# Matrix-product weights that begin 32 bytes later in SBUF, and two parts of the moving operand in swapped places

## The chip, the core and the metric

One core of a Trainium2 chip runs the whole program. TensorE (PE in the profile; its weight loads are listed apart as PEld) multiplies, VectorE (DVE), ScalarE (ACT) and GpSimd (POOL) do the elementwise work, SyncE (SP) issues transfers. The metric is device microseconds for one execution.

A matrix product on PE has two operands in SBUF: the weights (`lhsT`), which a weight load brings into the array before the product starts, and the moving operand (`rhs`), which streams through it, one column after the other. The weights of the next product are loaded while the present one streams, so two places of SBUF are read at a time.

## The reference

```python
def sm_attn(qq, kk, vv):
    s = scale * np.matmul(qq, kk.transpose(0, 1, 3, 2))
    s = s - np.max(s, axis=-1, keepdims=True)
    a = np.exp(s)
    a = a / (np.sum(a, axis=-1, keepdims=True) + 1e-09)
    return np.matmul(a, vv)
p_packed = sm_attn(p, k, v)          # p: (8, 8, 32, 64); q, k, v: (8, 8, 576, 64)
x = sm_attn(q, p_packed, p_packed)   # heads are then put side by side: (8, 576, 512)

h = x.transpose(0, 2, 1) @ U @ V     # U: (576, 32), V: (32, 576)
u = x + h.transpose(0, 2, 1)
out = u + np.maximum(u @ w_ch1, 0.0) @ w_ch2    # w_ch1: (512, 2048), w_ch2: (2048, 512)
```

## The kernel before

The work has an opening, in which the eight batches' packed keys and values are attended to, weights are read and converted, and batches 0 and 1 are begun; then a stage for batch 1; then a loop over batches 2 to 7, whose steps are written out in order (`prologue`, `batch_steps`, `joint_steps`, each word a step). The order on every engine is the order of these lists: nothing is scheduled behind the author's back. Each round of the loop computes the attention of the next batch beside the two large products of the present one.

**First product.** `half1` (L781) computes a piece of the hidden layer: for each of the two groups of heads, g = 0 and 1, three products by `mm3` (L98). Every number is split into a high and a low float32r part, and high x high, high x low, low x high are added; they stand at L100, L101 and L102. The weights are `wh` and `wl` (tiles `wth`, `wtl`, three buffers each), the moving operand is the attention weights `ah`, `al` (two buffers each). A tile of a is 1,152 numbers long and holds four parts: for each g 320 columns (r = 0) and 256 columns (r = 1). `part` (L90) gives the place of each. L419 and L441 are the two small products that mix U and V in (`ua4` and `ms` as weights, `x`, `xh` and `vs` as moving operand).

**Second product.** For batch 0 and 1 `tile2` (L817) multiplies the hidden layer `h` as weights by `w2h`, `w2l`, 512 columns at a time, again at L100 to L102. From batch 2 on a scheme with seven products in place of eight is used: `Sweep.products` and `Sweep.add` (L1054), all at L1058, 256 columns at a time, with weights `h` and moving operands `w2h`, `w2l` and the sums `ta`, `tb`, `tc`, `td`, `te` and, late, `x`.

**Places in SBUF.** Tiles come from pools in the order in which they are asked for, each rounded up to 32 bytes. Four tiles named `gap0` to `gap3` are never used; they only take room, so that what follows begins at a chosen place. SBUF is full to the last 32 bytes. Start of a tile in bytes of the partition, and its remainder by 128, as built:

| Tile | Part in the products | Start | mod 128 |
|---|---|---|---|
| `wth`, `wtl` (3 + 3 buffers) | weights of the first product | 121,280 (first) | 64 |
| `h` (2) | weights of the second | 165,312 (first) | 64 |
| `ah`, `al` (2 + 2) | moving, first product | 146,816 (first) | 0 |
| `w2h0` and the other seven | moving, second | 58,752 (first) | 0 |
| `ta`, `tb`, `tc`, `td`, `te`, `x` | moving, second | all | 0 |
| `ua4`; `ms` | weights of L419; of L441 | 21,120; 145,792 | 0 |
| `xT` (with `xh`, `xJ` in its place) | moving in L321, L419; source rows | 133,568 | 64 |
| `e` (softmax of the second attention) | not read by PE | 138,688 | 64 |
| `e1` (in the trace `e`) | weights of the transposes L327 | 216,544 (first) | 96 |
| `ident` | moving in all transposes | 16,512 | 0 |

Every single weight matrix begins a multiple of 512 bytes behind its tile's start, so the remainder is the same for all of them.

**Softmax of the second attention.** `side`, `most`, `each`, `power`, `total` and `back` (L359 to L387): DVE finds the maxima over 32 numbers (L367), POOL subtracts them (L371), ACT takes the exponential, DVE the sums (L379), POOL multiplies by their reciprocals (L371 again). Maxima and sums have a tile each, `m` and `s`, of 18 numbers.

Of the kernel before, what the change touches and what calls it, by code (L numbers as in the profile page):

```python
# [9 lines left out]
F32 = mybir.dt.float32  # L10
# [10 lines left out]
def packed_attention_mixer_kernel(  # L21
# [28 lines left out]
    B, H, S, D = q.shape  # L50
# [4 lines left out]
    P = 128  # L55
# [9 lines left out]
    HALF = (slice(0, 5 * I), slice(5 * I, S))  # L65
# [23 lines left out]

    def part(t, g, r):  # L90
        n = HALF[r].stop - HALF[r].start
        c0 = n * g + (0 if r else 2 * (S - HALF[1].start))
        return t[:, c0:c0 + n]

    def copy(scalar):
# [9 lines left out]
    pipe = ctx.enter_context(tc.tile_pool(name="pipe", bufs=1))  # L105
# [223 lines left out]
            nc.tensor.transpose(t_ps[:I, o:o + P], src[:, LAST], ident)  # L329


    def attention(b, res):

        st = {}
# [28 lines left out]
            nc.vector.transpose(st["e", g][:, (0, 10)[r]:(10, 18)[r]], st["ss", g][r][:, :n])  # L363

        def most(g):
            m = st["m", g] = pipe.tile([P, S // 32], F32, name="m", bufs=1)
            nc.vector.tensor_reduce(m, st["e", g], axis=AX.X, op=ALU.max)  # L367

        def each(g, what, op):
# [5 lines left out]

        def total(g, k):
            if k == 0:
                s = st["s", g] = pipe.tile([P, S // 32], F32, name="s", bufs=1)
                nc.vector.tensor_reduce(s, st["e", g], axis=AX.X, op=ALU.add)  # L379
            elif k == 1:  # L380
                nc.vector.tensor_scalar_add(st["s", g], st["s", g], 1e-9)
            else:
                nc.vector.reciprocal(st["s", g], st["s", g])
# [63 lines left out]
        def high_mix2(g, hf):  # L447
            nc.scalar.copy(part(res[b][0], g, hf), st["aT", g][:, HALF[hf]])  # L448

        def low_mix2(g, hf):  # L450
            (ah, al), aT, ns = (part(t, g, hf) for t in res[b]), st["aT", g], HALF[hf]
            nc.gpsimd.tensor_tensor(al, aT[:, ns], ah.bitcast(F32), op=ALU.subtract)  # L452
# [4 lines left out]
        if b != 2:  # L457
            gh = list(product(range(2), range(2)))
            return {
                "a0": [load], "a1": [run(load_q, 1)],  # L460
                **{f"q{h}": [run(turn_q, g, h) for g in range(2)] for h in range(3)},
                **{f"q{h}a": [lambda scalar, g=g, h=h: turned_q(g, h, scalar) for g in range(2)] for h in range(3)},
                "s3": [run(scores_q, g) for g in range(2)],
                "s4": [run(side, g, r) for g, r in gh],
                "s5": [run(most, g) for g in range(2)],
                "s6": [run(each, g, "m", ALU.subtract) for g in range(2)],
                "s7": [run(power, g) for g in range(2)],
                "s8": [run(total, g, k) for g in range(2) for k in range(3)],
                "s9": [run(each, g, "s", ALU.mult) for g in range(2)],
                "sa": [run(back, g) for g in range(2)],  # L470
                "t0": [room],
                "t1": [run(tokens, k) for k in (0, 2, 4)],
                "t2": [run(split_tokens, k, False) for k in (0, 2, 4)],
                "t3": [run(split_tokens, k, True) for k in (0, 2, 4)],
                "x0": [mix1], "x1": [run(split_mix1, False)], "x2": [run(split_mix1, True)],
                "y0": [run(mix2, g, hf) for hf, g in gh],
                "y1": [run(add_mix2, g, hf) for hf, g in gh],
                "y2": [run(high_mix2, g, hf) for hf, g in gh],
                "y3": [run(low_mix2, g, hf) for hf, g in gh],
                "pu": [put],  # L480
            }
# [10 lines left out]
        def step_most(g):  # L492
            most(g)
            each(g, "m", ALU.subtract)

        def step_total(g):
            for k in range(3):
                total(g, k)
            each(g, "s", ALU.mult)
# [64 lines left out]

    def folded(f_ps, b, c, a, g, low):
        if not wt:
            pipe.tile([P, 16], F32, name="gap3", bufs=1)
        if (b, 2 * c + a) not in wt:
            wt[b, 2 * c + a] = tuple(
                pipe.tile([P, 2, QW // 2], F32R, name=f"wt{x}", tag=f"wt{x}", bufs=3) for x in "hl")  # L570
        hi, lo = wt[b, 2 * c + a]
        src = f_ps[g][:, QW // 2 * a:QW // 2 * a + QW // 2]
        if not low:
            nc.scalar.copy(hi[:, g], src)  # L574
        else:
            nc.vector.tensor_tensor(lo[:, g], src, hi[:, g].bitcast(F32), op=ALU.subtract)  # L576

    def fold(b, c):
        f_ps = fold_products(b, c)
        for a, g, low in product(range(2), range(2), range(2)):  # L580
            folded(f_ps, b, c, a, g, low)
# [80 lines left out]
    def a_back(u, part, bank):  # L662
        t_ps = ua[u]["b_ps", part] = bank()
        for kk in ((0, 1, 2, 3), (4,))[part]:
            turn_back(t_ps, ua[u]["e"], kk, P * (kk % 4))
# [60 lines left out]
    pools, kept = {}, {}  # L726
# [3 lines left out]
    def h_tile():  # L730
        return first_h.pop() if first_h else pools["B"].tile([P, 2, 7 * P], F32R, name="h", bufs=2)

    def close_sA():
        actx.close()
        pools["B"] = ctx.enter_context(tc.tile_pool(name="sB", bufs=2, reuse_waits="tile"))
        pools["B"].tile([P, 16], F32, name="gap0", bufs=1)
        first_h.append(h_tile())
        pools["B"].tile([P, 112], F32, name="gap1", bufs=1)

    def close_psA():  # L740
        pctx.close()
# [408 lines left out]
    def folded_one(n, low):  # L1150
        n, m = divmod(n, 4)
        folded(f00[n], n // NPC, n % NPC, m // 2, m % 2, low)
# [25 lines left out]
    }  # L1178
    stages = {name: map(lambda n, f=f: lambda *args: f(n, *args), count()) for name, f in units.items()}
    side = [attention(b, res) for b in range(2)]  # L1180
    stages.update((name, iter(fs + side[1][name])) for name, fs in side[0].items())
    stages.update((name, iter(fs)) for name, fs in {
# [5 lines left out]
    for word in opening.split():  # L1188
        name = word.rstrip("v") if word not in stages else word
        stage = next(stages[name])  # L1190
        if name in ("e0", "e1", "ge") and not pools:
            close_sA()
        if name == "G0" and "O" not in pools:
            close_psA()
        if name in either:
            stage(name == word)
        else:
            stage()
    ahead = attention(2, res)
    ahead.pop(0)()  # L1200
    steps = ahead
    last = kept["cur"]
    now = Batch(1)
    for kt in range(NK):
# [11 lines left out]
        if kt % 4 == 2:  # L1216
            n = NPC + kt // 4 + 1
# [96 lines left out]
    for x in ("", "n"):  # L1314
# [8 lines left out]
            "S" + x: [lambda f=f: stream_w1((f[1] + 1) % NPC) for f in folds[x] if f != (B - 1, 3)],  # L1323
        })
    coming = [attention(b, res) for b in range(3, B)]
    stages.update({name: [f for a in coming for f in a[name]] for name in coming[0]})
    stages = {name: iter(fs) for name, fs in stages.items()}
# [50 lines left out]
```

## Time and profile before

| What | us |
|---|---|
| Time, median of 3 runs | 767.47 |
| Lowest and highest | 766.36, 768.63 |
| The profiled execution's own time | 768.76 |
| Its span, first to last instruction | 766.4 |

| Engine | Busy us | Share of the span | Instructions |
|---|---|---|---|
| PE | 751.3 | 98% | 7,792 |
| PEld | 662.2 | 86% | 7,792 |
| DVE | 590.3 | 77% | 1,223 |
| ACT | 405.3 | 53% | 1,020 |
| POOL | 84.7 | 11% | 116 |

The mean granted clock of TensorE is 0.998. A group of instructions is given with its line, engine, operation, tiles (out<-in), shape and count, then its busy us and the mean ns of one, then the idle time before it and what ended it. Matrix products overlap, so the mean duration of one (281 ns, say) is longer than the distance at which they follow each other; that distance is read from the chain of waits or the timeline, where a row has a start, a length in us and a count: in the chain a piece's length runs to the start of the next piece.

### The profile page before, as it was taken

How to read it: one execution, taken by the hardware profiler on the slowest of the kernel's cores; microseconds unless marked ns; L12 is line 12 of the kernel's file. 1: busy time of each engine (PE TensorE's matmuls, PEld its weight loads, DVE VectorE, ACT ScalarE, POOL GpSimd, SP SyncE). 2: the span in 40 equal slices, each digit the busy share in tenths (PEclk: the TensorE clock that was granted, in tenths of full speed). 3: DMA queues.
4: the chain of work that ended last, by engine and by line, in shares of the span. 5: the costliest groups of instructions: out<-in, count | busy, mean ns of one | idle time of the engine just before them, and what ended most of it. 6: DMA issues, size and time to landing. Idle time of an engine off the chain costs nothing.

```text
span 766.4 us, 19548 instructions
## 1 busy us (share of the span) xinstructions
PE 751.3 (98%) x7792; PEld 662.2 (86%) x7792; DVE 590.3 (77%) x1223; ACT 405.3 (53%) x1020; POOL 84.7 (11%) x116
## 2 busy tenths in 40 slices
PE   8999999999999999999999999999999999999996
PEld 6666778887878889998999989998999999999996
DVE  4799799877787668867888778857886788755786
ACT  4788755553344645555454544555455555464442
POOL 1123111010101011100211002010201020100000
PEclk9999999999999999999999999999999999999999
DMA  9999985379112874766479474657464746563672
GB/s 319 350 353 303 309 219 155 110 244 283 39 68 74 259 215 139 220 197 200 152 225 255 144 241 139 196 174 238 150 183 172 239 148 178 173 231 104 203 220 74
DMA packets 105689, 151.24 MB, mean 197 GB/s; under 512 B 40448, under 2 KB 59904, under 8 KB 102016
## 3 DMA queue, kind: packets, MB, share of 16 engines
q1 hardware_dynamic: 105440, 149.75, 62.0%
q8 instruction: 61, 1.00, 0.5%
q10 hardware_dynamic: 160, 0.26, 0.1%
q14 instruction: 28, 0.23, 0.1%
HBM read 116.29 MB, written 33.69 MB: 196 GB/s over the span
## 4 chain that ended last, share of the span: by engine, by line
PE 84%; DMA 5%; DVE 5%; ACT 3%; issue 1%; SPq 1%; POOL 0%; ACTq 0%; POOLq 0%; DVEq 0%
PE o L1058 32%; PE h_ps L100 9%; PE h_ps L101 8%; PE h_ps L102 8%; PE t_ps L562 4%; PE o L100 4%; PE o L101 3%; PE o L102 3%; DMA w1s<-w1D 2%; PE t_ps L301 1%; PE o L1080 1%; PE t_ps L321 1%; DMA bits<-in_moe_w_ch_dram 1%; PE t_ps L419 1%; PE t_ps L327 1%
## 5 line engine op out<-in xcount | busy, mean ns | idle before, releaser
L1058 PE MATMUL o<-w2h,h 128*128 128x256 f32 x896 | 178.9, 281 | 0.0
L100 PE MATMUL h_ps<-ah,wth 128*128 128x256 f32 (+1 forms) x512 | 157.6, 308 | 0.8 <-ACT aP L801 0.4
L101 PE MATMUL h_ps<-al,wth 128*128 128x256 f32 (+1 forms) x512 | 150.4, 294 | 0.0
L102 PE MATMUL h_ps<-ah,wtl 128*128 128x256 f32 (+1 forms) x512 | 150.3, 294 | 0.0
L1058 PEld LDWEIGHTS o<-w2h,h 128*128 128x128 f32 x896 | 146.4, 189 | 2.6 <-issue 2.6
L1052 DVE TENSOR_TENSOR h<-bits,h 128x896 fp32r<-128x896 f32 (+1 forms) x112 | 115.4, 1030 | 35.2 <-ACT h L1047 34.4
L1047 ACT CAST h<-bits 128x896 fp32r<-128x896 f32 (+1 forms) x112 | 100.4, 896 | 62.7 <-DVE bits L1035 37.7
L1058 PE MATMUL o<-w2l,h 128*128 128x256 f32 x448 | 125.0, 279 | 0.0
L100 PEld LDWEIGHTS h_ps<-ah,wth 128*128 128x128 f32 x512 | 96.4, 188 | 25.3 <-ACT ppall L1023 9.2
L101 PEld LDWEIGHTS h_ps<-al,wth 128*128 128x128 f32 x512 | 96.4, 188 | 1.0
L102 PEld LDWEIGHTS h_ps<-ah,wtl 128*128 128x128 f32 x512 | 96.4, 188 | 0.0
L1058 PE MATMUL o<-tb,h 128*128 128x256 f32 x504 | 88.0, 282 | 0.4 <-DVE h L1052 0.2
L1023 ACT ACTIVATE bits<-h_ps 128x256 f32<-128x256 f32 x132 | 49.4, 384 | 67.8 <-PE h_ps L102 50.8
L1058 PEld LDWEIGHTS o<-w2l,h 128*128 128x128 f32 x448 | 84.2, 188 | 0.0
L1058 PEld LDWEIGHTS o<-tb,h 128*128 128x128 f32 x504 | 71.9, 188 | 1.5 <-DVE h L1052 1.0
L576 DVE TENSOR_TENSOR wtl<-t_ps,wth 128x256 fp32r<-128x256 f32 x128 | 49.4, 418 | 29.4 <-ACT wth L574 28.3
L1033 DVE TENSOR_TENSOR bits<-bits 128x256 f32<-128x256 f32 x96 | 42.9, 447 | 26.3 <-ACT bits L1023 26.2
L574 ACT CAST wth<-t_ps 128x256 fp32r<-128x256 f32 x128 | 42.6, 376 | 26.5 <-PE t_ps L562 20.2
L452 POOL TENSOR_TENSOR al<-aT,ah 128x320 fp32r<-128x320 f32 (+1 forms) x32 | 31.3, 982 | 207.9 <-ACT ah L448 179.3
L100 PE MATMUL o<-w2h,h 128*128 128x512 f32 x128 | 52.1, 407 | 0.0
L101 PE MATMUL o<-w2l,h 128*128 128x512 f32 x128 | 50.6, 396 | 0.0
L102 PE MATMUL o<-w2h,h 128*128 128x512 f32 x128 | 50.6, 395 | 0.0
(178 smaller groups left out, 1307.7 us busy)
## 6 DMA issues: line engine op xcount, KB each, us to landing
w1s<-w1D SPq DMA_DIRECT2D x24, 1024.0 KB, 5.7
tc<-tD SPq DMA_DIRECT2D x94, 256.0 KB, 3.0
bits<-in_moe_w_ch_dram SPq DMA_DIRECT2D x32, 512.0 KB, 4.4
kx<-in_k_dram SPq DMA_DIRECT2D x16, 576.0 KB, 6.5
x<-in_q_dram SPq DMA_DIRECT2D x16, 576.0 KB, 5.9
vt<-in_v_dram SPq DMA_DIRECT2D x32, 256.0 KB, 6.1
out_dram<-os SPq DMA_DIRECT2D x32, 256.0 KB, 3.1
hD<-ppall SPq DMA_DIRECT2D x30, 256.0 KB, 4.2
```

What stands on the lines that cost most here:

```text
L100: nc.tensor.matmul(ps, lhsT=lh, rhs=rh, start=start, stop=False)
L101: nc.tensor.matmul(ps, lhsT=lh, rhs=rl, start=False, stop=False)
L102: nc.tensor.matmul(ps, lhsT=ll, rhs=rh, start=False, stop=stop)
L452: nc.gpsimd.tensor_tensor(al, aT[:, ns], ah.bitcast(F32), op=ALU.subtract)
L562: nc.tensor.matmul(f_ps[g][xs], lhsT=ppT[b][zs, g, xs], rhs=w[zs, h // 2], start=True, stop=True)
L574: nc.scalar.copy(hi[:, g], src)
L576: nc.vector.tensor_tensor(lo[:, g], src, hi[:, g].bitcast(F32), op=ALU.subtract)
L1023: nc.scalar.activation(dst[:, 256 * (i % 2):256 * (i % 2) + 256], src, AF.Relu)
L1033: vec(l[:, 4:6], s[:, 1:3], s[:, 0:1].to_broadcast([P, 2, P]), op=ALU.add)
L1047: nc.scalar.copy(h[:, ks], src)
L1052: nc.vector.tensor_tensor(lo[:, ks], src, h[:, ks].bitcast(F32), op=ALU.subtract)
L1058: nc.tensor.matmul(ps, lhsT=a, rhs=b, start=x not in self.begun, stop=last and i == 2)
```

## The change

Three things. The gap ahead of `wth` and the one ahead of `h` grow from 64 to 96 bytes, so that all weights of both large products begin 32 bytes later, at remainder 96; `gap1` behind `h` shrinks by as much, and what follows it stays in place. In the tiles of a the two parts of 320 columns swap places: g = 0 goes from +2,048 to +3,328 bytes and g = 1 from +3,328 to +2,048; the parts of 256 columns stay. And the maxima and sums of the softmax share one tile of 2 x 18 numbers, allocated once; that frees the 32 bytes which the gap ahead of `wth` takes, so that `aT0` and all that follows in the pool stay where they were.

```diff
     def part(t, g, r):
         n = HALF[r].stop - HALF[r].start
-        c0 = n * g + (0 if r else 2 * (S - HALF[1].start))
+        c0 = n * g if r else n * (1 - g) + 2 * (S - HALF[1].start)
         return t[:, c0:c0 + n]
...
+    few = []
+
...
         def most(g):
-            m = st["m", g] = pipe.tile([P, S // 32], F32, name="m", bufs=1)
+            if not few:
+                few.append(pipe.tile([P, 2, S // 32], F32, name="ms2", bufs=1))
+            m = st["m", g] = few[0][:, 0]
             nc.vector.tensor_reduce(m, st["e", g], axis=AX.X, op=ALU.max)
...
         def total(g, k):
             if k == 0:
-                s = st["s", g] = pipe.tile([P, S // 32], F32, name="s", bufs=1)
+                s = st["s", g] = few[0][:, 1]
...
         if not wt:
-            pipe.tile([P, 16], F32, name="gap3", bufs=1)
+            pipe.tile([P, 24], F32, name="gap3", bufs=1)
...
-        pools["B"].tile([P, 16], F32, name="gap0", bufs=1)
+        pools["B"].tile([P, 24], F32, name="gap0", bufs=1)
         first_h.append(h_tile())
-        pools["B"].tile([P, 112], F32, name="gap1", bufs=1)
+        pools["B"].tile([P, 104], F32, name="gap1", bufs=1)
```

No instruction is added, removed or moved: on all five engines the same operations stand in the same order with the same waits, and only addresses differ. As built:

| Tile | Start before | Start after | mod 128 before, after |
|---|---|---|---|
| `wth` (first) | 121,280 | 121,312 | 64, 96 |
| `wtl` (first) | 127,424 | 127,456 | 64, 96 |
| `h` (first, second) | 165,312, 172,480 | 165,344, 172,512 | 64, 96 |
| `xT`, `xh`, `xJ` | 133,568 | 133,600 | 64, 96 |
| `e` | 138,688 | 138,720 | 64, 96 |
| `m`, `s`; `ms2` | 140,992, 141,088 | 141,024 | 64, 32; 96 |

All other tiles stay.

## The prediction

> **What bounds the kernel now.** I read three views, from coarse to fine: the busy time of each engine in four stretches of the span, the groups of matrix products by line and shape, and the chain of waits in two windows. First the stretches; the columns are us, busy us of an engine and its instructions, granted clock, DMA share, GB/s.
>
> ```profile
> 0.00:260.00 260.00, 253.41 (x2696) 197.09 (x2696) 207.31 (x421) 150.08 (x414) 38.05 (x66) 1.00 0.69 219
> 260.00:430.00 170.00, 168.49 (x1760) 156.62 (x1753) 133.67 (x278) 87.71 (x209) 19.02 (x20) 1.00 0.66 201
> 430.00:700.00 270.00, 269.74 (x2685) 250.68 (x2685) 201.18 (x416) 141.06 (x349) 27.68 (x30) 1.00 0.58 183
> 700.00:766.40 66.40, 59.69 (x663) 57.77 (x661) 48.17 (x108) 26.46 (x49) 0.00 (x0) 0.98 0.53 159
> ```
>
> The first busy figure is PE. From 430 to 700 us it works 269.74 of 270 us, at a clock of 1.00; nothing else comes near (DVE 201). So no wait is to be won: the time is the number of matrix products times the distance at which they follow one another. Most of that work is products that are 256 columns wide.
>
> ```profile
> L1058 PE MATMUL o<-w2h,h 128*128 128x256 f32 x896 | 178.9, 281 | 0.0
> L1058 PE MATMUL o<-tb,h 128*128 128x256 f32 x504 | 88.0, 282 | 0.4 <-DVE h L1052 0.2
> L101 PE MATMUL h_ps<-al,wth 128*128 128x256 f32 x256 | 71.3, 279 | 0.0
> L101 PE MATMUL h_ps<-al,wth 128*128 128x320 f32 x256 | 79.0, 309 | 0.0
> L101 PE MATMUL o<-w2l,h 128*128 128x512 f32 x128 | 50.6, 396 | 0.0
> ```
>
> A product's own 281 ns say little, because products overlap. In the program there are 2,352 products of L1058 and 3 x 256 of L100 to L102 that are 256 wide (3,120 together), 768 that are 320 wide, and 384 that are 512 wide. The distance between them is read from the chain of waits: start, us until the next piece, what, and how many. These rows are two rounds of the batch loop, 78.17 us apart.
>
> ```profile
> 507.42 3.18 PE o L1058 x27
> 512.02 1.41 PE o L1058 x12
> 515.88 1.02 PE o L1058 x9
> 517.58 3.07 PE o L1058 x27
> 528.22 2.12 PE o L1058 x18
> 537.71 2.47 PE o L1058 x21
> 553.78 3.89 PE o L1058 x33
> 565.59 3.06 PE o L1058 x27
> 568.80 1.03 PE o L1058 x9
> ...
> 585.59 3.18 PE o L1058 x27
> 590.18 1.41 PE o L1058 x12
> 594.05 1.02 PE o L1058 x9
> 595.75 3.07 PE o L1058 x27
> ```
>
> This is what the case turns on. The same 27 products of the same shape take 3.18 us at 507.42 and 3.07 us at 517.58: 117.8 ns each and 113.5 ns each. 3.89/33, 2.47/21 and 2.12/18 are 117.8 again, 3.06/27 is 113.3, and nothing lies between. There are **two spacings**, a whole stretch holds one of them, and the next round has the same one at the same place (3.18, 1.41, 1.02, 3.07 in both). Counted over the start times of all 256-wide products, about 1,660 follow at the slow distance and 1,390 at the fast one; over long stretches the means are 117.80 and 113.38 ns, so 4.42 ns apart. No engine waits in either, and the clock is the same. What is left as a cause is how the two streams that PE reads, moving operand and next weights, meet in SBUF.
>
> **Whether the address has a part in it.** The change moves addresses and nothing else: the instructions of all five engines, their order and their waits are the same in both programs. So the question is what a distance of addresses costs. Weights and moving operand of the products above lie 64 bytes apart, modulo 128: ah, al, w2, ta to te at 0, wt and h at 64. The trace has one other case of the same shape and number form, L419 of the first three batches (moving x at 0, weights ua4 at 0).
>
> ```profile
> 230.72 1.19 PE t_ps L419 x10
> 231.91 0.15 PE h_ps L100
> ...
> 137.20 1.20 PE t_ps L419 x10
> ```
>
> 1.19/10 and 1.20/10: 119 to 120 ns, a third value, above both. So at distance 0 the product is slowest, and at 64 it has the two values. After the change the distance is 96, that is 32 from the next 0. For that distance the trace has one witness, of another form: transposes of 128 columns, those of L327 with weights e at 96 and moving ident at 0, those of L301 with weights x at 0 and the same ident.
>
> ```profile
> 66.34 0.60 PE L327 MATMUL m_ps<-ident,e 128*128 128x128 f32 x4
> 441.97 0.60 PE L301 MATMUL t_ps<-ident,x 128*128 128x128 f32 x4
> ```
>
> Four of them take 0.60 us in both places. So weights that begin 32 bytes off a multiple of 64 cost a transpose nothing, and the 0 costs it nothing either: in that form the two streams run at one pace and do not disturb each other. It speaks against a penalty for the start address by itself, and is silent on a product whose moving stream runs at twice the pace.
>
> **The change part by part.** The sum is made against the profiled execution: 768.76 us, a span of 766.4 us and 2.4 us around it. It lies 1.3 us above the median of 767.47 us; I add the differences to the median.
>
> *Weights 32 bytes later, 256-wide products.* From both sides: at best every slow product becomes a fast one, 1,660 x 4.42 ns = 7.3 us less. At worst the new distance acts as distance 0 does, and all go to 120.0 ns: 1,660 x 2.2 + 1,390 x 6.6 ns = 3.7 + 9.2 = 12.9 us more. Which is nearer? A product at distance 0 meets its next weights' stream at the very start and is slow without exception (three series of ten); at 64 it is fast in close to half the cases. I read this as a collision that is the cheaper the later it comes, and 96 puts it another 32 bytes later. That is one reading of two points, no more. By it the fast spacing is held from nearly everywhere. I don't take all of it: a stretch always opens with two or three products at the slow distance, and where PE waits for transfers a gain is partly waited away. The longest such wait in the whole run (us, times, longest):
>
> ```profile
> PE t_ps L562 <- DMA w1s<-w1D: 1.5, 2, 1.3
> ```
>
> So this part is small, and I take four fifths: 0.8 x 7.3 = **5.9 us less**.
>
> *Weights 32 bytes later, wider products.* The 320-wide and 512-wide ones have one spacing each; first the timeline of PE (start, us, what), then the chain.
>
> ```profile
> 434.00 0.31 PE L101 MATMUL h_ps<-al,wth 128*128 128x320 f32 x1
> 434.15 0.31 PE L102 MATMUL h_ps<-ah,wtl 128*128 128x320 f32 x1
> 434.29 0.31 PE L100 MATMUL h_ps<-ah,wth 128*128 128x320 f32 x1
> 434.44 0.31 PE L101 MATMUL h_ps<-al,wth 128*128 128x320 f32 x1
> ...
> 435.47 0.31 PE L102 MATMUL h_ps<-ah,wtl 128*128 128x320 f32 x1
> ```
>
> ```profile
> 215.84 0.23 PE o L100
> 218.17 0.23 PE o L101
> ```
>
> Ten steps from 434.00 to 435.47 are 147 ns each, ten from 215.84 to 218.17 are 233 ns each. Per column that is 0.459 and 0.455 ns, the same as the slow 117.8/256 = 0.460, and the fast spacing is 0.443. Here the weights have long been loaded when the products end, so I cost these at nothing. If they too went to the fast rate of 0.443, they would give 768 x 5 ns + 384 x 6.5 ns = 3.8 + 2.5 = 6.3 us; if they went to 120.0/256 = 0.469, they would cost 768 x 3 + 384 x 7 ns = 5.0 us. Both ends stay for the range.
>
> *The two parts of a.* In the rows from 434.00 the first two products (g = 0) read at +2,048 of the tile and those from 434.29 on (g = 1) at +3,328, which differ by 256 modulo 512: 0.15, 0.14, 0.15, 0.15 us. Neither place is dearer, so the swap is worth nothing by itself. It can shift which spacing the products behind it fall into, a matter of the item above.
>
> *Maxima and sums in one tile.* The same 16 reductions and 32 GpSimd instructions with the same waits. If the sharing made the next maximum wait for the last use of the sums, that use would be this row, 16 x 1.2 us, on an engine that is idle nine tenths of the time while PE has other products queued; at nothing.
>
> ```profile
> L371 POOL TENSOR_TENSOR e<-e,s 128x576 f32<-128x576 f32 x16 | 19.4, 1212 | 80.9 <-DVE s L383 65.8 <-DMA ppTd<-ppTa 4.8 <-ACT h L795 4.8
> ```
>
> *Writers of the moved tiles.* ACT and DVE now write wt, h, xT and e at addresses 32 bytes past a multiple of 64. ACT writes eT at such addresses already, and kT at multiples of 64:
>
> ```profile
> L310 ACT COPY kT<-k_ps 128x512 f32<-128x512 f32 x26 | 15.2, 589 | 2.8 <-PE k_ps L301 1.8 <-ACT two L701 0.7
> L672 ACT COPY eT<-m_ps 128x512 f32<-128x512 f32 x9 | 5.2, 583 | 0.0
> ```
>
> 589 and 583 ns: nothing. The sum: 767.5 - 5.9 = **761.6 us**.
>
> **A floor that a page gives.** The Trainium skill, "TensorE: Matmul & The Clock Gate", section "Back-to-back issue gap", puts the isolated distance at N/2.4 + 2.5 ns, which is 109.2 ns for 256 columns. If the change brought all of them there, 1,660 x 8.6 + 1,390 x 4.2 ns = 20 us would go and the time would be near 747 us; that is an estimate from the page, no stretch of this trace comes below 113.3 ns, and it is no end of my range.
>
> **The rivals.** *No effect (0.20).* The spacing is chosen by the moment at which a stretch begins, not by the address: for it speaks that a place in the round always repeats its value (3.18 at 507.42 and 585.59, 3.07 at 517.58 and 595.75), although ah and al change buffers from round to round. Against it speaks the 119 to 120 ns of L419 at distance 0. The time: 767.5 us, within 0.3% (2.3 us), about what a measurement can tell from no change. The Trainium skill comes to the same on another way: the same page, section "Step-by-step: what each phase is for", gives PE two independent SBUF read ports, so that loading the next weights takes no bandwidth from the running product. By that rule there would be one spacing per shape; the trace has 113.4, 117.8 and 120, so I give it no more than this chance.
>
> *Slower (0.28).* The phase at which the collision comes is worse at 96 than at 64, because 96 is only 32 bytes from the next multiple of 128, the distance that the trace shows to be slowest. Then the fast spacing is lost: it decides from the point where the stretches that are fast now (517.58, 565.59) read 3.18 us and not 3.07. Price: 1,390 x 4.42 ns = 6.1 us, so **773.6 us**; with all at 120.0, 780.4 us. For it: distance 64 is the farthest from 0 that a period of 128 allows, and the trace has nothing at 96 in this form.
>
> *Faster by more (0.12).* The wide products go to the fast rate too: 7.3 + 6.3 = 13.6 us, 753.9 us. Against it: in 768 of them no second spacing is to be seen now.
>
> That the change doesn't do what it says can be left out: in the built program wt lies at 121,312 and h at 165,344, both 32 bytes on.
>
> **How the numbers follow.** The forecast, a gain of 2.3 to 7.3 us, has 0.40; more than that 0.12; no effect 0.20; slower 0.28. So faster by over 0.3% has 0.52, within 0.3% 0.20, slower 0.28. The likeliest case by itself reaches from 760.0 to 765.2 us. The range takes in most of both sides: from 755.0, which leaves out the last of the wide products' gain, to 775.0, which takes in the loss of all fast spacings and leaves out the 120.0.
>
> **What would show it.** Right: in the chain, the 27 products that took 3.18 us take 3.07, and those of 3.07 stay; the group means of L1058 fall from 281 towards 277 ns, while L100 to L102 of 320 and 512 columns stay at 309 and 396. No effect: both values stand at the same places. Wrong on the slower side: 3.18 or 3.24 at 517.58's place in the round. The waits of PE should stay as they are (1.5 us for w1s, the longest); if they grow by microseconds, a faster PE has met a transfer, and my four fifths were too many. If the stretches swap values, some to fast and some to slow, the address sets the value but not in the way that I read it, and the sum is then only their count.

## The result and the profile after

| What | Before | After |
|---|---|---|
| Median of 6 runs, us | 768.04 | 773.14 |
| Lowest and highest, us | 766.36, 769.64 | 771.91, 775.63 |
| Ratio to before, 95% interval | | 1.0070 [1.0048, 1.0093] |
| Profiled execution, us; its span | 768.76; 766.4 | 773.0; 771.0 |

The change costs 0.5 to 0.9% where I had forecast a gain of 0.8%. The time is that of the rival "slower" (773.6 us), and so, within 0.01 us, is the sign it was to be known by (3.18 or more at 517.58's place in the round): the chain of waits of after, at the places of the round that were shown of before (start, us until the next piece, what, count).

```profile
509.51 3.21 PE o L1062 x27
514.14 1.42 PE o L1062 x12
518.03 1.06 PE o L1062 x9
519.79 3.17 PE o L1062 x27
530.63 2.14 PE o L1062 x18
540.16 2.47 PE o L1062 x21
556.26 3.92 PE o L1062 x33
568.19 3.21 PE o L1062 x27
571.55 1.05 PE o L1062 x9
...
588.27 3.21 PE o L1062 x27
592.90 1.42 PE o L1062 x12
596.79 1.06 PE o L1062 x9
598.55 3.17 PE o L1062 x27
```

L1062 is L1058 of before, four lines further down. The stretches that took 3.07 and 3.06 us now take 3.17 and 3.21, and 3.18 has become 3.21. So there are again two spacings, 3.17/27 = 117.4 ns and 3.21/27 = 118.9 ns, and neither of the old ones (113.4 and 117.8) is left. Over long stretches the means are 117.3 and 118.7 ns. A round takes 588.27 - 509.51 = 78.76 us in place of 78.17: 0.59 us more, and there are six rounds.

The groups by line and shape hardly show it, since a product's own duration is mostly overlap:

```profile
L1062 PE MATMUL o<-w2h,h 128*128 128x256 f32 x896 | 182.1, 282 | 0.0
L101 PE MATMUL h_ps<-al,wth 128*128 128x320 f32 x256 | 79.1, 309 | 0.0
L101 PE MATMUL o<-w2l,h 128*128 128x512 f32 x128 | 50.6, 395 | 0.0
```

Busy time of the first group has grown from 178.9 to 182.1 us; the wide products stand at 309 and 395 ns as they did at 309 and 396. In the stretches of the span the same 270 us hold 2,676 products in place of 2,685, with PE busy without a gap and the clock at 1.00:

```profile
430.00:700.00 270.00, 270.00 (x2676) 251.40 (x2669) 199.92 (x415) 140.59 (x348) 27.78 (x30) 1.00 0.57 183
700.00:771.00 71.00, 64.50 (x693) 62.82 (x692) 50.17 (x112) 28.18 (x53) 0.00 (x0) 0.97 0.50 153
```

PE's waits (us, times, longest) begin with these; the row of 1.5 us for `w1s` is gone.

```profile
PE t_ps L1132 <- DVE os L1129: 1.1, 1, 1.1
PE t_ps L700 <- DVE e L365: 0.6, 1, 0.6
```

**Where the 4.6 us of the span come from**, summed over the distances from each product's start to the next one's. Distances above 128.7 ns at 256 columns, 155.3 at 320 and 235.3 at 512, in either kernel, are put apart: most of them hold a wait or a change of stretch.

| Distances behind | After minus before, us |
|---|---|
| 256-wide products of L1062, weights h | +5.51 |
| 256-wide products of L100 to L102, weights wt | +1.78 |
| 320- and 512-wide products | +0.38 |
| the distances put apart | -3.15 |
| all else (transposes, small products, start and end) | +0.14 |
| Span | +4.65 |

So the products themselves lose 7.3 us at 256 columns. The bound at 512 columns runs through ordinary distances (about 230 to 239 ns), so that 171 of the 384 stand in the fourth row. Of the 3.1 us that come back 1.3 are one wait for `w1s` in the profiled execution of before. Six others that shrink by 0.2 to 0.4 us, two of them behind transfers and four ahead of L441, make 1.6. The rest, some shorter and some longer, come to 0.3. That a slower PE meets such waits less often is argued from this and not shown by a run of its own.

### The profile page after: what moved, and what is told of

Same layout as the page of the kernel before. It is cut to its first block, busy times and chain, and to the rows that moved or that the text cites. A ratio compares the mean times of both kernels' runs of the same rounds, so it can differ in the third digit from the quotient of the medians.

```text
span 771.0 us, 19548 instructions
## 1 busy us (share of the span) xinstructions
PE 757.5 (98%) x7792; PEld 668.7 (87%) x7792; DVE 590.2 (77%) x1223; ACT 405.7 (53%) x1020; POOL 84.8 (11%) x116
## 4 chain that ended last, share of the span: by engine, by line
PE 86%; DVE 5%; DMA 3%; ACT 3%; issue 1%; POOL 0%; SPq 0%; ACTq 0%; DVEq 0%
PE o L1062 35%; PE h_ps L100 9%; PE h_ps L102 8%; PE h_ps L101 8%; PE t_ps L566 4%; PE o L100 3%; PE o L102 3%; PE o L101 3%; DMA bits<-in_moe_w_ch_dram 2%; PE t_ps L301 1%; PE o L1084 1%; PE t_ps L321 1%; PE t_ps L423 1%; PE m_ps L700 1%; PE s_ps L321 1%
## 5 line engine op out<-in xcount | busy, mean ns | idle before, releaser
L1062 PE MATMUL o<-w2h,h 128*128 128x256 f32 x896 | 182.1, 282 | 0.0
L100 PE MATMUL h_ps<-ah,wth 128*128 128x256 f32 (+1 forms) x512 | 157.7, 308 | 0.7 <-ACT aP L805 0.4
L102 PE MATMUL h_ps<-ah,wtl 128*128 128x256 f32 (+1 forms) x512 | 151.0, 295 | 0.0
L1062 PEld LDWEIGHTS o<-w2h,h 128*128 128x128 f32 x896 | 146.8, 188 | 2.6 <-issue 2.6
L1062 PE MATMUL o<-w2l,h 128*128 128x256 f32 x448 | 125.6, 280 | 0.0
L100 PEld LDWEIGHTS h_ps<-ah,wth 128*128 128x128 f32 x512 | 96.4, 188 | 25.4 <-ACT ppall L1027 9.2
L102 PEld LDWEIGHTS h_ps<-ah,wtl 128*128 128x128 f32 x512 | 96.3, 188 | 0.0
L1062 PE MATMUL o<-tb,h 128*128 128x256 f32 x504 | 88.5, 283 | 0.3 <-DVE h L1056 0.2
L1062 PEld LDWEIGHTS o<-w2l,h 128*128 128x128 f32 x448 | 84.5, 189 | 0.0
L375 POOL TENSOR_TENSOR e<-e,ms 128x576 f32<-128x576 f32 x32 | 39.1, 1223 | 337.8 <-DVE ms L371 258.1
L1062 PEld LDWEIGHTS o<-tb,h 128*128 128x128 f32 x504 | 72.3, 189 | 1.2 <-DVE h L1056 1.0
L100 PE MATMUL o<-w2h,h 128*128 128x512 f32 x128 | 52.2, 408 | 0.0
L102 PE MATMUL o<-w2h,h 128*128 128x512 f32 x128 | 50.8, 397 | 0.2 <-DVE h L810 0.2
```

What stands on the lines that cost most here:

```text
L100: nc.tensor.matmul(ps, lhsT=lh, rhs=rh, start=start, stop=False)
L102: nc.tensor.matmul(ps, lhsT=ll, rhs=rh, start=False, stop=stop)
L375: nc.gpsimd.tensor_tensor(e, e, st[what, g].unsqueeze(2).to_broadcast([P, S // 32, 32]), op=op)
L1062: nc.tensor.matmul(ps, lhsT=a, rhs=b, start=x not in self.begun, stop=last and i == 2)
```

## The experiments

Three theories were to be told apart. **Distance**: the spacing depends on how far the weights lie from the moving operand, modulo 128 bytes, in each product by itself. **Start address**: weights off a multiple of 64 bytes are slow wherever the moving operand lies. **The other parts**: the swap in a, or the shared tile of the maxima and sums. Below, "spacing" is the mean distance of start to start of the 256-wide products with the distances put apart left out; P1 are the products with weights wt (L100 to L102), P2 those with weights h (L1058). Before has 115.61 ns in P1 and 115.91 in P2, after 118.07 and 118.32. P2 has 2,352 such products, P1 768.

**One part at a time.** Only h moves by 32 bytes:

```diff
-        pools["B"].tile([P, 16], F32, name="gap0", bufs=1)
+        pools["B"].tile([P, 24], F32, name="gap0", bufs=1)
...
-        pools["B"].tile([P, 112], F32, name="gap1", bufs=1)
+        pools["B"].tile([P, 104], F32, name="gap1", bufs=1)
```

> Only the hidden layer h, the weights of the second product, begins 32 bytes later (distance to the moving operand 96 modulo 128); wt, a and the softmax tiles are those of before. Theory 1, the distance sets the spacing of each product by its own weights: the 256-wide products of L1058 lose the 113.4 ns and show 117.3 or 118.7 ns everywhere, those of L100 to L102 keep stretches at 113.4; the time rises by about three quarters of the change's 5.1 us, to some 772 us. Theory 2, the swap of a's parts is what costs: as before, 768 us. Theory 3, any change of places only reshuffles which stretch gets which of the old two values (113.4, 117.8): both values are still there, the time within 2 us of 768.

Measured: 773.36 us, 1.0052 [1.0031, 1.0072]. The spacing is 118.49 ns in P2 and 115.91 in P1. The chain of waits:

```profile
509.86 3.21 PE o L1058 x27
520.13 3.24 PE o L1058 x27
556.55 3.92 PE o L1058 x33
```

And the timeline of PE, first and last of twelve products in a row with weights wt (start, us, what), of before and then of this kernel:

```profile
495.79 0.28 PE L100 MATMUL h_ps<-ah,wth 128*128 128x256 f32 x1
...
497.04 0.28 PE L102 MATMUL h_ps<-ah,wtl 128*128 128x256 f32 x1
```

```profile
498.37 0.28 PE L100 MATMUL h_ps<-ah,wth 128*128 128x256 f32 x1
...
499.62 0.28 PE L102 MATMUL h_ps<-ah,wtl 128*128 128x256 f32 x1
```

No stretch of P2 is fast any more (3.21 and 3.24, 3.92/33 = 118.8 ns), while P1 keeps its fast spacing next to it: 1.25 us for eleven steps in both kernels, 113.6 ns. Moving h alone makes the whole loss, as far as it can be measured.

Only wt moves, with the shared tile that makes room for it:

```diff
-            pipe.tile([P, 16], F32, name="gap3", bufs=1)
+            pipe.tile([P, 24], F32, name="gap3", bufs=1)
...
+                few.append(pipe.tile([P, 2, S // 32], F32, name="ms2", bufs=1))
```

> Only wt, the weights of the first product, begins 32 bytes later (with maxima and sums in one tile, to keep what follows in place); h and the order of a's parts are those of before. Theory 1 (distance): the 256-wide products of L100 to L102 lose the 113.4 ns; there are 768 of them against 2,352 of L1058, so the time rises by about a quarter of 5.1 us, to some 769.5 us. Theory 2 (swap): 768 us. Theory 3 (reshuffle): 113.4 and 117.8 at other places, within 2 us of 768.

Measured: 769.72 us, 1.0007 [0.9995, 1.0019]; P1 118.90 ns, P2 115.54. Chain of waits, then timeline at the same twelve products:

```profile
507.91 3.09 PE o L1062 x27
518.03 3.07 PE o L1062 x27
554.23 3.77 PE o L1062 x33
565.96 3.18 PE o L1062 x27
```

```profile
496.36 0.28 PE L100 MATMUL h_ps<-ah,wth 128*128 128x256 f32 x1
...
497.68 0.28 PE L102 MATMUL h_ps<-ah,wtl 128*128 128x256 f32 x1
```

The mirror image: P1 goes to 1.32 us for eleven steps, 120.0 ns, and P2 keeps both of its spacings. By the starts P1 loses 2.4 us, and it can't be seen in the time: P2 gains 0.9 us, because at some places its stretches changed value (3.09 where before had 3.18, 3.77 where it had 3.89), and the distances put apart are 1.9 us shorter.

Only the swap in a:

```diff
-        c0 = n * g + (0 if r else 2 * (S - HALF[1].start))
+        c0 = n * g if r else n * (1 - g) + 2 * (S - HALF[1].start)
```

> Only the two 320-column parts of a change places. Theory 1 (distance): the spacings stay 113.4 and 117.8 ns, since all distances modulo 128 stay, and the time is 768 us within 1 us; single stretches behind 320-wide products may swap values. Theory 2 (swap): 772 to 773 us. Theory 3 (reshuffle): the two values stand at other places, 766 to 770 us.

Measured: 769.40 us, 1.0005 [0.9989, 1.0020]; P1 115.70, P2 115.87 ns. The chain shows both old values at their old places:

```profile
510.69 3.18 PE o L1058 x27
520.85 3.07 PE o L1058 x27
```

The change without the swap, which is the first two diffs together:

> The change without the swap: both weights 32 bytes later, maxima and sums in one tile, a's parts as before. Theory 1 (distance): as the change, 773 us, no stretch at 113.4 ns. Theory 2 (swap): 768 us. Theory 3 (reshuffle): between 766 and 774 us, with the values 117.3 and 118.7 at other places than in the change.

Measured: 773.56 us, 1.0057 [1.0036, 1.0079]; P1 118.14, P2 118.22 ns, as after. The swap and the shared tile are out of it. What is left is one of the two address theories.

**Other distances for h.** The same two gaps, with 8 and 120 (h at 32 modulo 128):

> h alone begins 32 bytes earlier: distance 32 to the moving operand, everything else as before. If the nearness to the next multiple of 128 sets the spacing, 32 acts as 96: 117.3 and 118.7 ns in all L1058 stretches, 772 to 773 us. If what costs is that the weights begin off a multiple of 64 bytes, the same. If the order in which the two streams reach a place matters, 32 differs from 96: below 117 or above 119 ns, 768 us or less, or 775 us or more.

Measured: 773.27 us, 1.0057 [1.0040, 1.0074]; P2 118.28 ns. And with 32 and 96 (h at 0, on a multiple of 128):

> h alone at distance 0 (64 bytes later than before), on the 64-byte grid. If the distance modulo 128 sets the spacing: 120 ns as in L419, that is 2,352 x 4.1 ns = 9.6 us more, 778 us. If only a start off a multiple of 64 costs: 113.4 and 117.8 ns as before, 768 us.

Measured: 772.67 us, 1.0046 [1.0032, 1.0060]; P2 118.59 ns. At the place where before has its fast 3.07, the chain of the one and then of the other has

```profile
519.66 3.20 PE o L1058 x27
```

```profile
519.68 3.20 PE o L1058 x27
```

Weights on a multiple of 128 bytes are as slow as those 32 bytes off: a start off a multiple of 64 is not the cause. At distance 0 neither of the two forecasts came out, 778 or 768 us: every stretch is slow, but the mean is 118.6 ns and not 120.

**The same distance from the other side.** The weights stay on their multiple of 64 and a, the moving operand of P1, goes 32 bytes earlier (to 96), so the distance of wt from a is 96 as in after:

```diff
+                few.append(pipe.tile([P, 2, S // 32], F32, name="ms2", bufs=1))
...
                 res[b] = tuple(pipe.tile([P, 2 * S], F32R, name=f"a{x}", tag=f"a{x}", bufs=2) for x in "hl")
+                if b == 0:
+                    pipe.tile([P, 8], F32, name="gap4", bufs=1)
```

> wt as before (64), but a, its moving operand, begins 32 bytes earlier (96 modulo 128): the distance is 96, and the weights stand on the 64-byte grid. Only the first product (L100 to L102, 256 columns) is looked at. If the distance counts: 117 to 120 ns, no 113.4. If the weights' start off the grid counts: 113.4 and 117.8 ns.

Measured in one run: 768.93 us, beside 767.76 to 770.40 (10 runs) of before. P1 117.97 ns, P2 115.27. Timeline of twelve products with weights wt:

```profile
397.78 0.28 PE L100 MATMUL h_ps<-ah,wth 128*128 128x256 f32 x1
...
399.07 0.28 PE L102 MATMUL h_ps<-ah,wtl 128*128 128x256 f32 x1
```

Eleven steps take 1.29 us, 117.3 ns, one of the two values of after. By their starts, none of the program's 26 series of eleven or twelve such products has a mean below 117.0 ns; in before 19 of them lie at 113.2 to 113.5, their first three steps left out. Moving the moving operand does what moving the weights does. The distance between the two accounts for both; so would a rule that wants the weights at 64 and the moving operand at 0, each by itself. The next kernel parts the two.

Now wt 32 bytes earlier and a 32 bytes earlier: distance 64, but weights at 32 and moving operand at 96.

```diff
+                if b == 0:
+                    pipe.tile([P, 8], F32, name="gap4", bufs=1)
...
-            pipe.tile([P, 16], F32, name="gap3", bufs=1)
+            pipe.tile([P, 8], F32, name="gap3", bufs=1)
```

> wt begins 32 bytes earlier (32 modulo 128) and a 32 bytes earlier too (96): the distance is 64 as before, but both stand off the 64-byte grid. First product only. If the distance counts: 113.4 and 117.8 ns. If the grid counts: 117 to 120 ns.

Measured in one run: 769.12 us; P1 117.55 ns, P2 114.96. This bears out the distance in part. 24 of the 26 series of P1 stand at 117.7 to 117.8 ns, and the other two change to 113.3 ns on the way; here are the last seven products of one of them, six steps in 0.68 us.

```profile
454.20 0.28 PE L102 MATMUL h_ps<-ah,wtl 128*128 128x256 f32 x1
...
454.88 0.28 PE L102 MATMUL h_ps<-ah,wtl 128*128 128x256 f32 x1
```

So the fast value occurs with neither operand in its old place, but it is rare, where before has it in 19 series of 26. P2, whose tiles did not move, is fast more often than before, and at other places of the round:

```profile
508.23 3.06 PE o L1060 x27
518.31 3.18 PE o L1060 x27
529.12 2.04 PE o L1060 x18
```

3.06 and 3.18 have changed places, and 18 products take 2.04 us where they took 2.12. Distance 64 allows the fast spacing; which stretch gets it is settled by something else.

The single steps, by the starts in whole ns, show more than the means. In the kernel just described a series of P1 reads 118, 117, 118, 118, 118, 117, 119, 117, 118, 118, 117; in the one before it, at distance 96, a series reads 117, 118, 117, 115, 118, 117, 120, 117, 115, 118, 117. At 64 the steps are even, whichever of the two values they hold. In series of eight steps or more at most 12 of 100 steps fall outside 112 to 114 and 117 to 119 ns, for P1 and P2 of every kernel in this document that has distance 64, and for P1 of this one 1 of 100. At every other distance it is at least 41 of 100. By this sign the products with weights at 32 and moving operand at 96 belong to distance 64: the distance counts, and the places by themselves don't.

**How narrow is it.** h 16 bytes to either side of its place, by tiles of h that are 128 bytes longer and used from their fifth number on:

```diff
-        return first_h.pop() if first_h else pools["B"].tile([P, 2, 7 * P], F32R, name="h", bufs=2)
+        return first_h.pop() if first_h else pools["B"].tile([P, 14 * P + 32], F32R, name="h", bufs=2)[:, 4:4 + 14 * P].rearrange("p (z n) -> p z n", z=2)
...
-        pools["B"].tile([P, 112], F32, name="gap1", bufs=1)
+        pools["B"].tile([P, 48], F32, name="gap1", bufs=1)
```

That is distance 80; for 48 `gap0` is 8 numbers and `gap1` 56.

> h alone, 16 bytes later than before: distance 80 to the moving operand; everything else as before. If the good distance is a narrow place at 64: 117 to 119 ns in all L1058 stretches, as at 96, 772 to 773 us. If it is a region around 64 that 96 and 32 just miss: 113.4 ns in half or more of the stretches, 765 to 769 us. If a 16-byte line is what counts, 80 is like 64.

> h alone, 16 bytes earlier than before: distance 48. If the good distance is a narrow place at 64: 117 to 119 ns in all L1058 stretches, 772 to 773 us. If it is a region around 64: 113.4 ns in half or more of the stretches, 765 to 769 us. If only the later side of 64 is good (or only the earlier), this one and the one at 80 differ.

Measured: 80 gives 770.89 us, 1.0029 [1.0015, 1.0043], P2 117.85 ns; 48 gives 771.52 us, 1.0043 [1.0027, 1.0060], P2 118.07 ns. Chains of 80 and of 48, at the place of the fast 3.07:

```profile
518.17 3.19 PE o L1058 x27
```

```profile
517.33 3.19 PE o L1058 x27
```

Sixteen bytes in either direction are enough to lose 113.4 ns everywhere: the good place is narrow. The times lie some 0.5 to 1 us below the 772 to 773 that went with it. Finally h a whole 128 bytes later (`gap0` 48, `gap1` 80), distance 192, which is 64 again modulo 128:

> h alone, 128 bytes later than before: distance 192, which is 64 modulo 128; everything else as before. If the distance counts modulo 128: L1058 shows 113.4 and 117.8 ns again, in some mixture, and the time lies within 3 us of 768. If its period is longer than 128: 117 to 119 ns everywhere, 772 to 773 us.

Measured: 769.23 us, 1.0008 [0.9995, 1.0021]; P2 116.94 ns.

```profile
508.00 3.18 PE o L1058 x27
518.21 3.06 PE o L1058 x27
543.69 1.03 PE o L1058 x9
```

Both old values are back (3.06/27 = 113.3 ns), and the time is that of before within the interval. Fewer stretches are fast: of the steps in series of eight or more about 340 of 1,944, before some 910 of 1,938. Taken together:

| Distance of h from its moving operand, mod 128 | Spacing of P2, ns | Means of series of eight steps or more, ns | Ratio of the time |
|---|---|---|---|
| 0 | 118.59 | 117.5 to 120.3 | 1.0046 [1.0032, 1.0060] |
| 32 | 118.28 | 117.8 to 118.6 | 1.0057 [1.0040, 1.0074] |
| 48 | 118.07 | 117.8 to 118.8 | 1.0043 [1.0027, 1.0060] |
| 64 (before) | 115.91 | 113.3 to 117.9, most near 113.4 or 117.8 | 1 |
| 64 (192) | 116.94 | 113.2 to 118.4, most near 113.4 or 117.8 | 1.0008 [0.9995, 1.0021] |
| 80 | 117.85 | 116.7 to 118.9 | 1.0029 [1.0015, 1.0043] |
| 96 | 118.49 | 117.2 to 120.4 | 1.0052 [1.0031, 1.0072] |

The ratio of the time is less than the spacing alone would make it (at 48: 2,352 x 2.16 ns = 5.1 us, measured 3.4), for the reason given of after: a slower PE waits less. Each spacing comes from one profile. The three kernels with h at 96 have 118.22 to 118.49, and the six with h at 64 have 114.96 to 116.94, so that 64 stands clear of the others, while their order among themselves is hardly clear of the scatter. No kernel that was run is faster than before.

## Why the prediction was wrong

**The step that failed** is the item on the 256-wide products: "I read this as a collision that is the cheaper the later it comes, and 96 puts it another 32 bytes later." It was drawn as a slope through two points, 0 and 64. The runs show no such slope but one narrow good place: 64 has the 113.4 ns, and 0, 32, 48, 80 and 96 do not have it in h. Past 64 there is no more to be had; 16 bytes past it the fast value is gone (117.85 ns). No run shows the collision itself. The term that followed, 1,660 slow products gaining 4.42 ns with four fifths taken, had the wrong sign: the slow ones did not become fast, the fast ones became slow. The reason given for the four fifths, that a stretch always opens with two or three products at the slow distance, was misread too: of the 42 fast series of P2 in before (eight steps or more) 19 are fast from their first step. Two slips in its sums change nothing: the likeliest case reaches down to 760.2 us and not 760.0 (767.5 - 7.3), and the 512-wide products would gain 6.2 ns each and not 6.5 (233 ns less 512 x 0.443).

**The rival "slower" named what happens and where**: the fast stretches, at 3.18 us or more (3.17 and 3.21 came). Its reason holds in part. "64 is the farthest from 0 that a period of 128 allows" agrees with 192 being like 64; but a cost that follows the nearness to a multiple of 128 does not fit 48 and 80, which are 48 bytes from one and nearly as slow as 0 (118.07 and 117.85 against 118.59 ns). Its size, 1,390 x 4.42 = 6.1 us, was the loss of the fast value alone. The slow value also moved, to 117.3 and 118.7, so the products lost 7.3 us; of that 3.1 came back in the distances put apart. That 6.1 us lies so near the measured 5.1 (768.04 to 773.14) is in part two errors that cancel.

**No effect** is excluded by the interval, and with it the idea that only the moment at which a stretch begins decides. A part of it holds: at distance 64 both values occur with the same addresses, and the runs with other tiles moved (wt alone, a and wt) changed which stretch has which. The row that bears on the ports is 3.24 us against 3.07 for the same 27 products with h moved by 32 bytes, with no wait and at a clock of 0.998 in both profiles. By the rule cited in the prediction (the Trainium skill, "TensorE: Matmul & The Clock Gate", "Step-by-step: what each phase is for": two independent read ports, weight loads take nothing from the running product) both would read alike; the runs disagree, by 3.24/3.07, which is 5.5%. Whether it is at the ports that the two streams disturb each other, no run shows.

**The points that held.** PE bounds the kernel and a wait is not to be won. Spacings that a whole stretch holds were the right thing to count. The wide products, costed at nothing, lost 0.4 us. The swap and the shared tile are worth nothing (1.0005 for the swap alone; the shared tile is part of the kernel that moves only wt, 1.0007). GpSimd's 32 instructions on the shared tile take 39.1 us, 1,223 ns each, as they did apart:

```profile
L375 POOL TENSOR_TENSOR e<-e,ms 128x576 f32<-128x576 f32 x32 | 39.1, 1223 | 337.8 <-DVE ms L371 258.1
```

The cover for waits held too: none of PE's waits has grown by microseconds.

**The witness from transposes misled.** Four of them take 0.60 us at 96 and at 0 alike, and I read that as no penalty for a start 32 bytes off. It was right as far as it went, since h on a multiple of 128 bytes is slow too, so that the start by itself is not the cause; but it said nothing of the distance in the products that matter, as the text noted, and then the forecast went on as if it had. That the two streams of a transpose run at one pace stands in no row either: the trace has 109 ns from one of these products to the next and 141 ns for a weight load. The other witness, L419 at distance 0 with 119 to 120 ns, was a good one: P2 at distance 0 came to 118.59, with stretches up to 120.

**What stays open.** Why 64 is good, that is, what inside PE or SBUF the two streams share, no trace shows. Nor does one show why the steps are even there. What selects the fast or the slow value at 64 was not found; no run changed the start of a stretch without changing addresses. Whether the 64-byte grid makes fast stretches rarer stays open as well: the one run off it (weights at 32, moving operand at 96) had few in P1, and 192, which is on it, had few in P2.

## What to carry to other kernels

Where PE is the bound and products of one shape show more than one spacing with no wait between them, look at where the weights begin relative to the moving operand, and sweep that distance in small steps through a whole period before reading a trend out of two places. Change it for one pair of operands at a time and read the result from stretches of equal products in the chain of waits; the mean duration of a product (281 against 282 ns) hides it. Don't price the loss by count alone: here 3.1 of the 7.7 us that all products lost came back in the distances that hold waits.

## What was not expected of the hardware

Sixteen bytes decide: h at distance 64 runs stretches at 113.4 ns, at 48 and at 80 none of eight steps or more below 116.7. Products of one shape follow each other without a wait at 113.4 or 117.8 ns where the steps are even, at 64; at 96 the means of long stretches are 117.3, 118.7 and 120.0 ns, the first two made up of steps from 115 to 122. And the swap of which stretches are fast by moving tiles that those products don't read (P2 at 115.54 and 114.96 ns in the kernels that moved only wt, or wt and a, against 115.91) was not foreseen by any of the theories.
